# Transposing u on VectorE in blocks of 32 by 32, by way of DRAM, instead of on TensorE

## Chip, core and metric

One core of a Trainium2 chip. The metric is the device time of one execution in microseconds (us). Every time quoted with a ratio is the median of several executions, all of the fast state. Four runs were executed once only, so that their state is unknown; they are marked "one look". The experiments ran in sets on four chips, each beside runs of the kernel before on the same chip (831.6 to 831.8 us in each set).

## The reference, cut to what matters

Float32 throughout. An attention without softmax feeds an MLP mixer: first over tokens, then over channels.

```python
kv  = einsum('bhsd,bhse->bhde', k, v)
out = einsum('bhsd,bhde->bhse', q, kv)
x   = rms_norm(out) * g_norm            # (8, 576, 512), heads side by side
u   = x + (relu(x^T @ w_tok1) @ w_tok2)^T
res = u + relu(u @ w_ch1) @ w_ch2       # w_ch1: 512 x 1536, w_ch2: 1536 x 512
```

The second pass of the kernel is the last line. It works on nine groups of 512 tokens.

## The kernel before

The matmuls of this kernel sum over partitions, so `u @ w_ch1` needs u with its features on partitions; u lies in DRAM with tokens on partitions. The kernel before loads a tile of 128 tokens and turns it with four 128x128 transposes on TensorE, and ScalarE copies the result out of PSUM:

```python
def fetch_t(g, i):
    xt[g, i] = late["xt"].tile([P, DM], F32, name="xt")     # two buffers
    dma(xt[g, i], u_dram[g][ts(i, P)])

def turn_u(g, i, psum):                   # four times a group
    if i == 0:
        uT[g] = late["u"].tile([P, 7, 7, P], F32, name="uT")
    pt = psum()
    for c in range(NC):                   # NC = 4
        keep(nc.tensor.transpose(pt[:, c], xt[g, i][:, ts(c, P)], ident))
    o, n = 2 * (i // 2), 2 * (i % 2)
    copy(uT[g][:, o:o + 2, n:n + 2], pt.rearrange("p (o n) t -> p o n t", o=2))
```

Both channel matrices are multiplied by a fast scheme on two levels: seven products instead of eight, each of which is seven products again. So a group is 2 x 7 x 7 = 98 inner products of six matmuls. One inner product is one *place* of a hand-made schedule: `put(place, step)` lays a step of another engine behind the matmuls of that place. Places b to b+48 of the first channel matrix are the *first half* of a group, the 49 of the second its *second half*. Each engine's instructions stand in this order in the traces, also where one of them waits.

An outer product shares its PSUM banks between inner products. Bank `a` gathers four of them, and between two of them another engine reads the running sum:

```python
PLACE = {1: 0, 2: 1, 6: 3, 5: 4, 7: 6, 4: 9, 3: 12}
def read(o, i, j):
    a = fit(banks["a"], to(i, j))
    if base: tensor_add(o, a, base(i, j))     # VectorE
    else:    copy(o, a)                       # ScalarE
at(1, "a", True, False, lambda: read(temp("t1", 1), 0, 0))
at(6, "a", False, False, lambda: read(temp("u2", 2), 0, 1))   # next product into bank a
...                                                           # must wait for this read
```

A read that comes late on VectorE therefore stops TensorE. The second half has operands of its own (`sv`, sums of parts of v) made by VectorE shortly before TensorE needs them; its schedule, and the transposes of the next group in it:

```python
for place, steps in (
        ...
        (11, [ins[6][0]]), (12, [S4[0]]), (13, [ins[6][1], S4[1]]), ...   # S4: n3 = n2 - n6, 128x768
        (36, [xadd(0, 1, 5), ins[3][1]]), (37, [xadd(1, 1, 5)]), ...
        (44, [xadd(1, 0, 7)]), (45, [xadd(1, 1, 7)])):                    # additions to u
    put(b + place, *steps)
for i in range(J):                                                        # J = 4
    place = b + 12 + 4 * i
    put(place - 12, do(fetch_t, g + 1, i)) if i < 2 else None
    put(place - 1, do(turn_u, g + 1, i, t_psum))
    put(place, do(fetch_t, g + 1, i + 2)) if i < 2 else None
```

## Time and profile before

| | before |
|---|---|
| time | 831.66 us, median of 3 (831.65 to 831.73) |
| profiled span, granted clock | 830.2 us, 0.999 |
| first product of group 0 / first of group 1 starts | 206.34 / 280.73 us |
| first half of a group (groups 2 to 8) | 32.83 us = 49 places x 0.67 |
| second half | 34.96 us |
| TensorE waits inside groups 2 to 8 | none that the trace shows |

The halves are read from the timeline of TensorE: the start of one marker product to the start of the next. A first half of 32.83 us is TensorE at its own pace without a gap. The second half holds the four transpose sets besides (4 x 0.44 = 1.76 us), and 32.83 + 1.76 = 34.59, so 0.37 us more than its matmuls explain. Keep that in mind; it became the second half of this story. The lines of the page are in the prediction below.

### The profile page before, as it was taken

To read this page: it belongs to the slowest core of one execution; us is meant where nothing else is said; L and a number is where in the kernel's file an instruction comes from. 1 tells how busy PE (TensorE), PEld (TensorE's weight loads), DVE (VectorE), ACT (ScalarE), POOL (GpSimd) and SP (SyncE) were. 2 spreads that over 40 slices of the span, in tenths; PEclk is the share of its full clock that TensorE was granted. 3 is DMA by queue.
4 is the path that set the end of the run, shared out by engine and by line. 5 is a ranking of instruction groups with operands and counts; after the bars stand their busy time and mean duration, and the time that the engine had idled before them with its cause. 6 is when DMAs were issued, how large, how long until landed. Compare 5 with 4: busy or idle time off the path is not lost.

```text
span 830.2 us, 16562 instructions
## 1 busy us (share of the span) xinstructions
PE 812.6 (98%) x6528; PEld 719.9 (87%) x6528; DVE 701.8 (85%) x1334; ACT 289.1 (35%) x777; POOL 76.9 (9%) x59
## 2 busy tenths in 40 slices
PE   6999999999999999999999999999999999999997
PEld 6655555644888899999999999999999999999997
DVE  4688989999785979978977987997897897798696
ACT  1346665562210124234234323322423322333321
POOL 1200101010000020003003003001100300300300
PEclk9999999999999999999999999999999999999999
DMA  9999996422436445365356446546536545644642
GB/s 296 325 341 319 337 364 244 153 89 102 174 127 220 175 169 170 118 194 200 128 165 216 144 141 204 181 140 193 192 115 191 185 149 145 216 164 141 190 144 80
DMA packets 67966, 156.57 MB, mean 189 GB/s; under 512 B 5296, under 2 KB 24752, under 8 KB 67888
## 3 DMA queue, kind: packets, MB, share of 16 engines
q1 hardware_dynamic: 66208, 153.77, 56.6%
q10 hardware_dynamic: 1680, 1.74, 0.7%
q8 instruction: 52, 0.85, 0.4%
q14 instruction: 26, 0.21, 0.1%
HBM read 128.35 MB, written 27.13 MB: 187 GB/s over the span
## 4 chain that ended last, share of the span: by engine, by line
PE 88%; DVE 9%; issue 1%; DMA 1%; ACT 1%; SPq 0%; ACTq 0%; DVEq 0%
PE ps_a L127 35%; PE ps_b L127 18%; PE ps_c L127 9%; PE ps_h L127 6%; PE ps_u L127 6%; PE ps_v L127 4%; PE ps_w L127 3%; PE ps_o L127 3%; PE ps_ut L515 2%; PE ps_kv L127 2%; DVE sv L118 1%; DMA raw<-in_moe_w_tok_dram 1%; DVE v L118 1%; DVE x L379 1%; DVE ms L399 1%
## 5 line engine op out<-in xcount | busy, mean ns | idle before, releaser
L124 ACT COPY u<-ps_a 128x128 f32<-128x128 f32 (+1 forms) x176 | 60.5, 344 | 176.5 <-PE ps_a L127 164.6
L118 POOL TENSOR_TENSOR v<-v,v 128x768 f32<-128x768 f32 x32 | 58.4, 1856 | 553.0 <-ACT t L124 553.0
L127 PE MATMUL ps_b<-uT,sums 128*128 128x128 f32 x672 | 85.5, 275 | 0.0
L127 PEld LDWEIGHTS ps_b<-uT,sums 128*128 128x128 f32 x672 | 80.2, 192 | 0.0
L127 PE MATMUL ps_a<-uT,w_ch 128*128 128x128 f32 x576 | 78.8, 275 | 0.0
L127 PEld LDWEIGHTS ps_a<-uT,w_ch 128*128 128x128 f32 x576 | 71.5, 192 | 0.1
L118 DVE TENSOR_TENSOR v<-ps_b,u 128x384 f32<-128x384 f32 x112 | 60.2, 550 | 12.9 <-PE ps_b L127 12.9
L127 PE MATMUL ps_u<-h,w_tok 128*128 128x512 f32 (+1 forms) x160 | 67.0, 601 | 0.0
L127 PE MATMUL ps_h<-x,w_tok 128*128 128x512 f32 (+1 forms) x160 | 65.8, 603 | 0.8 <-ACT x L424 0.8
L118 DVE TENSOR_TENSOR v<-v,v 128x768 f32<-128x768 f32 (+1 forms) x70 | 64.1, 926 | 0.3
L118 DVE TENSOR_TENSOR uT<-uT 128x512 f32<-128x512 f32 (+4 forms) x103 | 63.1, 628 | 1.1
L124 ACT COPY t<-ps_a 128x128 f32<-128x128 f32 (+1 forms) x88 | 30.3, 344 | 92.7 <-PE ps_a L127 85.3
L121 ACT ACTIVATE v<-v 128x384 f32<-128x384 f32 (+1 forms) x102 | 49.3, 526 | 30.7 <-DVE v L118 26.6
L127 PE MATMUL ps_a<-uT,w 128*128 128x128 f32 x432 | 58.7, 275 | 0.0
L118 DVE TENSOR_TENSOR u<-ps_a,v 128x384 f32<-128x384 f32 x48 | 26.8, 558 | 32.1 <-PE ps_a L127 31.6
L127 PEld LDWEIGHTS ps_h<-x,w_tok 128*128 128x128 f32 (+1 forms) x160 | 25.9, 189 | 31.9 <-issue 28.1
L127 PEld LDWEIGHTS ps_a<-uT,w 128*128 128x128 f32 x432 | 53.4, 192 | 0.0
L118 DVE TENSOR_TENSOR xg<-xg,r 128x512 f32<-128x512 f32 (+1 forms) x78 | 50.7, 661 | 0.8 <-ACT r L124 0.6
L424 ACT ACTIVATE x<-x,inv 128x64 f32<-128x64 f32 x184 | 46.0, 335 | 9.5 <-DVE inv L419 8.1
L127 PE MATMUL ps_a<-uT,sums 128*128 128x128 f32 x336 | 46.9, 276 | 1.3 <-ACT t L124 1.3
L127 PE MATMUL ps_a<-sums,sv 128*128 128x128 f32 x336 | 47.3, 277 | 0.9 <-ACT r L124 0.5
L127 PEld LDWEIGHTS ps_u<-h,w_tok 128*128 128x128 f32 (+1 forms) x160 | 24.5, 179 | 27.1 <-issue 22.4
(123 smaller groups left out, 1650.1 us busy)
## 6 DMA issues: line engine op xcount, KB each, us to landing
sums<-sums SPq DMA_DIRECT2D x112, 576.0 KB, 3.8
qT<-in_q_dram SPq DMA_DIRECT2D x8, 1152.0 KB, 9.5
xt<-u_dram SPq DMA_DIRECT2D x36, 256.0 KB, 3.5
xg<-u_dram SPq DMA_DIRECT2D x18, 512.0 KB, 4.9
k_in<-in_k_dram SPq DMA_DIRECT2D x16, 512.0 KB, 9.2
u_dram<-x SPq DMA_DIRECT2D x16, 512.0 KB, 3.6
out_dram<-xg SPq DMA_DIRECT2D x16, 512.0 KB, 5.4
sums<-sv SPq DMA_DIRECT2D x14, 576.0 KB, 2.8
```

The source lines that it names most:

```text
L118: keep(engine.tensor_tensor(out=o, in0=a, in1=b, op=op))
L121: keep(nc.scalar.activation(o, a, AF.Relu))
L124: keep(nc.scalar.copy(o, a))
L127: keep(nc.tensor.matmul(*a, **kw))
L379: keep(nc.vector.tensor_mul(heads(X[pair, c][:, t]), heads(bank[c, t]), g_sb.to_broadcast([P, H, D])))
L399: keep(nc.vector.tensor_reduce(stats_of(c)[0][:, ts(t, H)], sq[c, t], axis=AX.X, op=ALU.add))
L424: keep(nc.scalar.activation(x[:, i], x[:, i], AF.Copy, scale=inv[:, i]))
L515: keep(nc.tensor.transpose(pt[:, c], xt[g, i][:, ts(c, P)], ident))
```

## The change

The intent: take 144 transposes off the engine that is busy 98% of the time. VectorE transposes each tile within blocks of 32 by 32, and two trips through DRAM put the blocks into their place. `uT` gets another layout (tokens in runs of 32). The loading and turning moves from the second half of the group before into its first half, four additions to u go into the next group in return, and the two PSUM banks of the transposes go to the products.

```diff
-    for c in range(NC):
-        keep(nc.tensor.transpose(pt[:, c], xt[g, i][:, ts(c, P)], ident))
-    copy(uT[g][:, o:o + 2, n:n + 2], pt.rearrange(...))
+def turn_blocks(g, i):
+    half, n = i // 2, 2 * (i % 2)
+    if n == 0:
+        xt[g] = late["y" if g else "y0"].tile([P, NC, 2, NC, Q], F32, name="y")   # one buffer
+    for o in range(2):
+        keep(nc.vector.transpose(xt[g][:, :, o, n:n + 2]..., xt[g, i][:, ts(o, DH)]...))
+    if n:                                              # after each second tile
+        t = blocks_dram[g, half] = dram.tile([Q, NC, 2, NC, P], F32, ...)
+        for a in range(NC):
+            dma(t[:, :, :, a], xt[g][ds(a * Q, Q)]...)
+def fetch_u(g, half):
+    for b in range(NC):
+        dma(uT[g][ds(b * Q, Q), 2 * half:2 * half + 2, :, :4]..., blocks_dram[g, half][:, b])
 ...
+        for place, f, i in ((2, fetch_t, 0), (8, turn_blocks, 0), (10, fetch_t, 1), (14, turn_blocks, 1),
+                            (16, fetch_t, 2), (20, turn_blocks, 2), (22, fetch_t, 3),
+                            (26, turn_blocks, 3)):
+            put(b + place, do(f, g + 1, i))            # first half
 ...
-   (36, [xadd(0, 1, 5), ins[3][1]]), (37, [xadd(1, 1, 5)]), ... (44, [xadd(1, 0, 7)]), (45, [xadd(1, 1, 7)])
+   (36, [ins[3][1]]), ... (53, [xadd(1, 1, 5)]), (55, [xadd(1, 0, 7)]), (56, [xadd(1, 1, 7)]), (59, [xadd(0, 1, 5)])
-        (transposes of group g + 1 at b + 11, 15, 19, 23)
+        put(b + 8, do(fetch_u, g + 1, 0))              # second half
+        put(b + 10, do(fetch_u, g + 1, 1))
-    late["xt"] = pool("xt", 2)
+    late["xt"] = pool("xt", 1)
-    late["m"] = pool("m", 6, PSUM); late["t"] = pool("t", 2, PSUM)
+    late["m"] = pool("m", 8, PSUM)
```

(Cut; group 0 and group 1 have their own placing: group 0 is turned during the last token mixing, group 1 during the single product stage between.)

More of the change, by code (lines that the diff above doesn't have):

```diff
@@ L504, in fetch_t @@
         if g < NG:
-            xt[g, i] = late["xt"].tile([P, DM], F32, name="xt")
+            xt[g, i] = late["xt" if g else "xt0"].tile([P, DM], F32, name="xt")
             dma(xt[g, i], u_dram[g][ts(i, P)])
-    def turn_u(g, i, psum):
+    Q = 32
+    blocks_dram = {}
+    def turn_blocks(g, i):
         if g >= NG:
             return
-        if i == 0:
-            uT[g] = late["u"].tile([P, 7, 7, P], F32, name="uT")
-        pt = psum()
-        for c in range(NC):
-            keep(nc.tensor.transpose(pt[:, c], xt[g, i][:, ts(c, P)], ident))
-        o, n = 2 * (i // 2), 2 * (i % 2)
-        copy(uT[g][:, o:o + 2, n:n + 2], pt.rearrange("p (o n) t -> p o n t", o=2))
+        half, n = i // 2, 2 * (i % 2)
+        if n == 0:
+            xt[g] = late["y" if g else "y0"].tile([P, NC, 2, NC, Q], F32, name="y")
+        for o in range(2):
+            keep(nc.vector.transpose(
+                xt[g][:, :, o, n:n + 2].rearrange("p b n t -> p n b t"),
+                xt[g, i][:, ts(o, DH)].rearrange("p (n b t) -> p n b t", n=2, b=NC)))
+        if n:
+            t = blocks_dram[g, half] = dram.tile([Q, NC, 2, NC, P], F32, name=f"blocks{g}{half}")
+            for a in range(NC):
+                dma(t[:, :, :, a], xt[g][ds(a * Q, Q)].rearrange("p b o n t -> p b o (n t)"))
+    def fetch_u(g, half):
+        if g >= NG:
+            return
+        if half == 0:
+            uT[g] = late["u"].tile([P, 7, NC, 7, Q], F32, name="uT")
+        for b in range(NC):
+            dma(uT[g][ds(b * Q, Q), 2 * half:2 * half + 2, :, :4].rearrange("p o a n t -> p o a (n t)"),
+                blocks_dram[g, half][:, b])
     def outer_u(g):
-        return t_sums(lambda n: uT[g][:, SB[n], :4]) if g < NG else []
+        return t_sums(lambda n: uT[g][:, SB[n], :, :4]) if g < NG else []
     def inner_u(g, lo, hi):
-        return t_sums(lambda n: uT[g][:, lo:hi, SB[n]]) if g < NG else []
+        return t_sums(lambda n: uT[g][:, lo:hi, :, SB[n]]) if g < NG else []
     V = {}
@@ L530, in m_psum @@
         return late["m"].tile(shape, F32, name=name, tag="m")
-    def t_psum():
-        return late["t"].tile([P, NC, P], F32, name="ps_ut")
     def v_tile(g, i):
@@ L568, in product @@
                         matmul(ps[:, w], lhsT=wt[:, 2 * i + c, ts(f, P)],
-                               rhs=uT[g][:, SB[n], c:4:2],
+                               rhs=uT[g][:, SB[n], :, c:4:2].rearrange("p a n t -> p n a t"),
                                start=(start and w == 0 and c == 0), stop=stop,
@@ L762, in mul @@
                     matmul(ps[:, ts(w, P)], lhsT=part(1, o, p, sums[n])[:, ts(w, P)],
-                           rhs=uT[g][:, SB[o], SB[p]], start=(start and w == 0), stop=stop,
+                           rhs=uT[g][:, SB[o], :, SB[p]], start=(start and w == 0), stop=stop,
                            skip_group_check=True)
@@ L881, in channel2 @@
                 (28, [ins[2][0]]), (29, [radd(6, 1)]), (30, [ins[2][1], xadd(0, 1, 6)]),
-                (32, [ins[2][3], ins[2][2]]), (34, [ins[3][0]]), (36, [xadd(0, 1, 5), ins[3][1]]),
-                (37, [xadd(1, 1, 5)]), (38, [ins[3][3], ins[3][2]]), (43, [radd(7, 6)]),
-                (44, [xadd(1, 0, 7)]), (45, [xadd(1, 1, 7)])):
+                (32, [ins[2][3], ins[2][2]]), (34, [ins[3][0]]), (36, [ins[3][1]]),
+                (38, [ins[3][3], ins[3][2]]), (43, [radd(7, 6)])):
             put(b + place, *steps)
         if g < NG - 1:
-            for place, steps in ((57, [do(store, g, xg, 1)]), (59, [xadd(0, 0, 2)]), (63, [xadd(0, 1, 3)]),
+            for place, steps in ((53, [xadd(1, 1, 5)]), (55, [xadd(1, 0, 7)]), (56, [xadd(1, 1, 7)]),
+                                 (59, [xadd(0, 1, 5)]), (60, [do(store, g, xg, 1)]), (61, [xadd(0, 0, 2)]),
+                                 (64, [xadd(0, 1, 3)]),
                                  (71, [do(store, g, xg, 0)]), (78, [do(fetch_x, g + 1, 0)]),
@@ L896, in last @@
                 tensor_add(to, to, rs[3][0][:, m, ts(n, P)])
+            for place, step in ((36, xadd(0, 1, 5)), (37, xadd(1, 1, 5)), (44, xadd(1, 0, 7)), (45, xadd(1, 1, 7))):
+                put(b + place, step)
             put(b + 49, xadd(0, 0, 2), do(store, g, xg, 1))
@@ L901, in channel2 @@
             put(b + 56, do(last, 0, 1), do(store_rest, xg, 0))
-        for i in range(J):
-            place = b + 12 + 4 * i
-            put(place - 12, do(fetch_t, g + 1, i)) if i < 2 else None
-            put(place - 1, do(turn_u, g + 1, i, t_psum))
-            put(place, do(fetch_t, g + 1, i + 2)) if i < 2 else None
+        put(b + 8, do(fetch_u, g + 1, 0))
+        put(b + 10, do(fetch_u, g + 1, 1))
         if g + 1 < NG:
@@ L1043 @@
     late["xg"] = pool("xg", 1)
-    late["xt"] = pool("xt", 2)
+    late["xt"] = pool("xt", 1)
     late["u"] = pool("u", 1)
+    first = ExitStack()
+    late["xt0"] = pool("xt0", 2, stack=first)
+    late["y0"] = pool("y0", 2, stack=first)
     fetch_t(0, 0)
@@ L1049, with turn @@
     woven = fill[0][:4] + fill[1] + fill[0][4:]
-    def turn(g, i, psum):
-        turn_u(g, i, psum)
+    def turn(i):
+        turn_blocks(0, i)
         if i + 2 < J:
-            fetch_t(g, i + 2)
-    u_psum = lambda: ps["o"].tile([P, NC, P], F32, name="ps_ut", tag="o")
+            fetch_t(0, i + 2)
+        if i % 2:
+            fetch_u(0, i // 2)
     last = [
-        "h00 2 -s40 2", "h01 2", "h10 2", "h11 2", "hr 1", "c0 u0 1", "c1 u1 1", "c2 u2", "c3 u3 1", "u4",
-        "c4 u5 1", "u6 1", "u7", "u8"]
-    more = {f"c{i}": do(turn, 0, i, u_psum) for i in range(J)}
+        "h00 2 -s40 2", "h01 c0 2", "h10 c1 2", "h11 c2 2", "hr c3 1", "u0 1", "u1 1", "u2", "u3 c4 1", "u4 1",
+        "u5 1", "u6 1", "u7", "u8"]
+    more = {f"c{i}": do(turn, i) for i in range(J)}
     more[f"c{J}"] = lambda: [f() for f in outer_u(0)]
@@ L1066 @@
     right.close()
+    first.close()
     late["v"] = pool("v", 1, "right")
@@ L1073 @@
     late["d2"] = pool("d2", 1, "right").tile([P, 3, NS, DH], F32, name="d2")
-    late["m"] = pool("m", 6, space=bass.MemoryType.PSUM)
-    late["t"] = pool("t", 2, space=bass.MemoryType.PSUM)
+    late["y"] = pool("y", 1, "right")
+    late["m"] = pool("m", 8, space=bass.MemoryType.PSUM)
     fetch_x(0, 0)
     fetch_x(0, 1)
-    fetch_t(1, 0)
-    fetch_t(1, 1)
     firsts, lasts = mix_ch2()
@@ L1084 @@
     inner2 = [split(2, o) for o in ORDER2]
-    weave(channel1_once(0), firsts + [f for fs, _ in inner1 for f in fs])
+    sums1 = firsts + [f for fs, _ in inner1 for f in fs]
+    blocks1 = [do(f, 1, i) for f, i in (
+        (fetch_t, 0), (turn_blocks, 0), (fetch_t, 1), (turn_blocks, 1), (fetch_t, 2),
+        (turn_blocks, 2), (fetch_t, 3), (turn_blocks, 3))]
+    n = len(sums1) // len(blocks1)
+    fill = []
+    for i, step in enumerate(blocks1):
+        fill += [step] + sums1[n * i:n * i + n]
+    weave(channel1_once(0), fill + sums1[n * len(blocks1):])
     for n in range(3):
         fetch_sums(n)
-    extra = [do(turn, 1, i, t_psum) for i in range(J)]
-    extra += [lambda: [f() for f in outer_u(1)], lambda: [f() for f in inner_u(1, 0, 7)], lambda: None]
-    body = [step for pair in zip(channel2_once(0), extra) for step in pair]
+    extra = [lambda: (fetch_u(1, 0), fetch_u(1, 1)), lambda: None, lambda: None,
+             lambda: [f() for f in outer_u(1)], lambda: [f() for f in inner_u(1, 0, 7)]]
+    extra += [lambda: None] * (len(channel2_once_steps := channel2_once(0)) - len(extra))
+    body = [step for pair in zip(channel2_once_steps, extra) for step in pair]
     weave(body, lasts + [f for fs, _ in inner2 for f in fs] + [f for _, f in inner1])
```

## The prediction

> **What bounds the kernel now.** I read the page first: busy shares, the slices, the chain of work that ended last, the groups.
>
> ```profile
> PE 812.6 (98%) x6528; PEld 719.9 (87%) x6528; DVE 701.8 (85%) x1334; ACT 289.1 (35%) x777; POOL 76.9 (9%) x59
> ...
> PE 88%; DVE 9%; issue 1%; DMA 1%; ACT 1%; SPq 0%; ACTq 0%; DVEq 0%
> ```
>
> TensorE is busy 98% of an 830.2 us span at full clock; most of the missing 17.6 us is the start. So every TensorE instruction that goes is worth its own time, as long as nothing else then arrives late. Next the transposes, as a group with one row per shape:
>
> ```profile
> L515 PE MATMUL ps_ut<-ident,xt 128*128 128x128 f32 x144 | 21.7, 273 | 0.0
> ...
> L124 ACT COPY uT<-ps_ut 128x512 f32<-128x512 f32 x36 | 21.1, 587 | 42.4 <-PE ps_ut L515 42.4
> ```
>
> The mean (273 ns) is a latency; matmuls overlap. The cost on the path is the step from one start to the next, in the chain in order of time:
>
> ```profile
> 727.04 1.34 PE ps_a L127 x12
> 728.38 0.67 PE ps_b L127 x6
> 729.05 0.44 PE ps_ut L515 x4
> 729.49 0.77 PE ps_b L127 x6
> ```
>
> Four transposes take 0.44 us, six matmuls 0.67. The second pass has nine groups of 512 tokens; groups 1 to 8 are fourteen products of 42 matmuls each, and one group takes 67.79 us (the chain shows the same matmuls at 356.59 and 424.38). Then I cut group 3 into its two halves, and the first half into five stretches of seven places (one place = six matmuls = 0.67 us):
>
> ```profile
> core 0: us, PE busy (x) PEld busy (x) DVE busy (x) ACT busy (x) POOL busy (x), PEclk, DMA share, GB/s
> 415.90:449.70 33.80, 33.80 (x305) 33.80 (x305) 25.14 (x48) 11.39 (x26) 7.29 (x4) 1.00 0.57 182
> 449.70:483.70 34.00, 33.95 (x304) 33.72 (x303) 33.30 (x71) 11.33 (x35) 0.00 (x0) 1.00 0.49 158
> ...
> 416.85:421.55 4.70, 4.70 (x45) 4.70 (x44) 4.24 (x9) 1.49 (x4) 0.00 (x0) 1.00 0.37 84
> 421.55:426.25 4.70, 4.70 (x45) 4.70 (x44) 3.77 (x7) 1.92 (x4) 0.00 (x0) 1.00 0.56 191
> 426.25:430.95 4.70, 4.70 (x45) 4.70 (x44) 2.63 (x6) 0.96 (x2) 0.00 (x0) 1.00 0.39 126
> ```
>
> The reader is to see that VectorE, at 85% on average, is at 98% in the second half of a group (second channel matrix, where the transposes are) and at 74% in the first, and that within that first half the first ten microseconds are the fullest (8.0 of 9.4 us).
>
> [...] Here 256 KB loads of u land 2.5 to 7.2 us after issue, median 3.5.
>
> **The change, part by part.**
>
> Removed from TensorE: 144 transposes. 36 sets of 0.44 us = 15.8 us, all on the chain. This is the gross gain. ScalarE loses 36 copies of 0.587 us (21.1 us), and it was only 35% busy.
>
> Small waits in group 1: TensorE waits 1.29 us there, and the chain back from it runs over the sums of u on VectorE (1.90 us and 2.49 us). These sums now come one product earlier: up to -1.3.
>
> Added to VectorE: 9 groups x 4 tiles x 2 = 72 block transposes of 128x256. [...] each should cost what a 128x256 addition does here: 418 ns alone, about 0.35 us in a row. Eight a group = 2.8 us; 25 us in all.
>
> Moved: four additions to u (681 ns, 0.61 in a row) leave the crowded second half of a group for the first microseconds of the next: 2.4 us. The halves become about 25.1+2.4+2.8 = 30.3 and 33.3-2.4 = 30.9 us. Against 65.7 us of matmuls (98 places of 0.67) that fits on average. The order of instructions decides whether it fits in detail.
>
> *Second half.* From 449.94 to 462.2 VectorE has no idle time, and the operand sv of product 6 of the third set is finished at about 462.16 (0.55 us from 461.61); TensorE starts on it at 462.25. Up to there the changed kernel gives VectorE the same work: the four additions came later. The matmuls alone would be ready at 449.01 + 18 x 0.67 = 461.07. So two of the four transposes of a group are paid back as a wait of about 1.2 us, and only the other two (0.88 us) are gained.
>
> *First half.* Products whose partial sums go through an addition to an earlier block must be read by VectorE before TensorE may go on in that bank; the first such read is at place 14. In the changed order four more additions and one pair of transposes stand ahead of it: 2.4+0.7 = 3.1 us, where VectorE idled 0.21+0.72+0.78 = 1.7. So the read is about 1.4 us later; its slack was 0.6 (read done 427.66, next product 428.25): a wait of about 0.8. Before the next read stand another pair and one addition: about 0.7 more. Then the DMA: the third transpose pair needs a tile whose load is issued only behind four block writes: I estimate four issues of 0.35 plus some 3 us to land = 4.5 us or more after the second pair, against about 3.8 us of work between. The fourth has a single buffer again. That delays the read at place 28 by perhaps 0.8. Sum 1.5 to 2.3 us a group.
>
> So a group costs 65.7 + 1.2 + 1.5 to 2.3 = 68.4 to 69.2, against 67.8: over the six groups that have all of it, +4 to +8. Group 1 and the last have part of it: about 0.
>
> *Group 0.* -1.8 on TensorE. But eight transposes (2.8 us) enter a VectorE that is full (8.66 of 8.8 us from 180.0 to 188.8), and the first sums of u now wait for two transfers through DRAM, about 8 us behind the last transpose; the evictions behind them hold the four banks of the token mixing. Estimate: +1 to +3 net. The single product stage that follows gets group 1's transposes and loads: +1. The stage after it loses four sets: -1.8, and the -1.3.
>
> Sum of this schedule: 831.7 + (4 to 8) + (1 to 3) + 1 - 1.8 - 1.3 = 834.6 to 840.6.
>
> **Rivals.** *All of it hidden:* if VectorE's lag is absorbed (the change also raises the PSUM banks of the products from 6 to 8, and ScalarE's copies no longer stand ahead of its reads), the time is 831.7 - 15.8 - about 2 = 814. For it: average load fits, 61 of 65.7 us; someone placed the moved additions with care. Against: the in-order reads above. *Transposes slower than an addition* [...] 845 to 855. Nothing in the profile speaks for or against. *Transfers:* 16 more transfers a group on one queue, in rows of 512 bytes; if the weight sums, loaded on the same queue three products ahead, come late, TensorE waits on DMA. Their landing is 3.8 us and I count some 11 places (7.4 us) from issue to use, so this should stay hidden, but the mean DMA share is already 0.5. *Strided matmuls:* u is now read in runs of 32; a matmul with runs of 128 (ps_v, 380 ns) costs what a contiguous one does (ps_w, 379), so I take nothing for it.
>
> **Range and chances.** My schedule says 834 to 841, full hiding 814. A hand schedule counts each lag as fully exposed, so I weigh it at two thirds and the hidden case at one third: 837 x 2/3 + 814 x 1/3 = 829. Faster by over 2% (below 815.0) needs nearly the whole gross gain: 0.10. Slower by over 2% (above 848.3) needs slow transposes or late weights: 0.13. Within 2%: 0.77. Range 814.5 to 846.
>
> **What would show it.** Right: no ps_ut rows; TensorE waits (or stretched steps) at the reads ps_a<-... by VectorE in the first half, and for sv in the second; VectorE over 90% in both halves; transposes of about 0.42 us, some with a DMA wait ahead. Wrong: groups of 66 us with TensorE gapless (then the lag is absorbed), a transpose row far from 0.42 us, or TensorE waiting for sums.

## The result, and the profile after

| | before | after |
|---|---|---|
| median | 831.69 us (4 runs, 831.65 to 831.90) | 886.31 us (4 runs, 883.67 to 889.61) |
| profiled span, granted clock | 830.2 us, 0.999 | 887.8 us, 0.981 |
| first product of group 0 / of group 1 | 206.34 / 280.73 | 210.93 / 284.29 |
| first halves of groups 2 to 8 | 32.83 | 42.53, 41.04, 40.02, 39.60, 40.99, 37.59, 32.84 |
| second halves | 34.96 | 34.86 |

The ratio is 1.066 (95% interval 1.062 to 1.070). A ratio here is the mean time of one kernel's fast runs over that of the other's of the same rounds, so it is not quite the ratio of the medians.

So the kernel got 55 us slower, in two places. The first halves of groups 1 to 7 got longer: +44.8 us in groups 2 to 7, and +10.0 in group 1 (44.01 us from its first product to the first marker of its second half, against 34.03). The start of group 1 got 3.6 us later. With the second halves (seven times -0.1) that is the whole difference of the two spans, 57.6 us. The last group has no next one to turn, and its first half is gapless at 32.84. The second half, from which the 1.76 us of transposes were taken, gained 0.10 us.

The page of the changed kernel: first the busy row, then the chain's shares.

```profile
PE 823.1 (93%) x6384; PEld 719.6 (81%) x6384; DVE 723.4 (81%) x1406; ACT 268.4 (30%) x741; POOL 77.0 (9%) x59
...
PE 46%; DVE 34%; DMA 11%; issue 4%; SPq 3%; ACT 1%; DVEq 0%; ACTq 0%
```

The 144 matmuls are gone, and yet TensorE's busy time has *risen* by 10.5 us. In the chain, DMA went from 1% to 11% and VectorE from 9% to 34%. A TensorE that does less work in more time points to waits and to a slower clock (granted 0.981, against 0.999 before). The waits, longest in total first (engine and line, releaser: us in total, times, longest):

```profile
PE ps_a L127 <- DVE t L118: 18.5, 13, 5.2
PE ps_a L127 <- DMA sums<-sums: 8.9, 5, 2.4
PE ps_b L127 <- DVE v L118: 7.1, 8, 2.1
```

and VectorE's own, with the cost of the transposes themselves (a group by shape):

```profile
DVE y L521 <- DMA xt<-u_dram: 26.4, 14, 5.3
```

```profile
L521 DVE STREAM_TRANSPOSE y<-xt 128x256 f32<-128x256 f32 x72 | 27.5, 420 | 26.4 <-DMA xt<-u_dram 26.4
```

A transpose costs 420 ns, as predicted. What is dear is that it stands in VectorE's order and waits for its load. One first half (group 3, place b at 439.88 us) shows how. VectorE's transposes, two per tile (start, duration, what it waited for in brackets):

```profile
451.68 0.76 DVE L521 STREAM_TRANSPOSE y<-xt 128x256 f32<-128x256 f32 x2
...
458.17 0.77 DVE L521 STREAM_TRANSPOSE y<-xt 128x256 f32<-128x256 f32 x2 [1.72 <-DMA xt<-u_dram]
...
464.21 0.77 DVE L521 STREAM_TRANSPOSE y<-xt 128x256 f32<-128x256 f32 x2 [2.17 <-DMA xt<-u_dram]
```

the issues on the queue that carries all these transfers:

```profile
452.46 2.54 SPq L115 DMA_DIRECT2D blocks<-y  x4
455.11 0.55 SPq L115 DMA_DIRECT2D xt<-u_dram  x1
455.70 0.44 SPq L115 DMA_DIRECT2D sums<-sums  x1
...
458.97 0.32 SPq L115 DMA_DIRECT2D xt<-u_dram  x1
```

and the chain there, which is the same thing seen from its end:

```profile
455.11 2.94 DMA xt<-u_dram
...
458.97 5.22 DMA xt<-u_dram
```

The second tile is turned at 451.68. Only after four block writes, issued in 2.54 us, is the third tile's load issued; it lands 2.94 us later; VectorE turns it at 458.17. There is one buffer, so the fourth load can only go at 458.97, takes 5.22 us, and VectorE stands again until 464.21. Everything on VectorE behind these transposes is late too, among it the reads of bank `a` and the results of bank `b`. TensorE in the same stretch:

```profile
451.81 0.94 PE L127 MATMUL ps_a<-uT,sums 128*128 128x128 f32 x6 [0.37 <-DVE t L118]
...
459.44 0.94 PE L127 MATMUL ps_b<-uT,sums 128*128 128x128 f32 x6 [0.69 <-DVE v L118]
...
465.95 1.65 PE L127 MATMUL ps_a<-uT,sums 128*128 128x128 f32 x6 [2.89 <-DVE t L118]
467.39 2.77 PE L127 MATMUL ps_b<-uT,sums 128*128 128x128 f32 x12
469.95 2.42 PE L127 MATMUL ps_a<-uT,w 128*128 128x128 f32 x12
```

Where nothing waits in this half, twelve matmuls take 1.50 us as a row. After the wait of 2.89 us they take 2.77 and 2.42. From start to start, the 30 matmuls from 465.95 take 6.26 us in place of 30/6 x 0.67 = 3.35. The stretch 465 to 470 (window, then us, TensorE busy, weight loads, VectorE, ScalarE, GpSimd, granted clock, DMA share, GB/s) says why:

```profile
465.00:470.00 5.00, 4.05 (x19) 4.05 (x20) 3.78 (x8) 0.89 (x2) 0.00 (x0) 0.50 0.75 144
```

The granted clock was 0.50. So this first half is 41.04 - 32.83 = 8.2 us too long, of which 2.9 us is half clock after a long wait and 5.3 us is waits (stretched steps at 451.8, 454.5, 459.4 and 466.0: about 0.6, 0.6, 1.0 and 3.1). Over the whole run the clock was 0.50 in six stretches of 3.41 or 6.83 us, and TensorE worked in 27.7 us of them. Half of that, 13.9 us, is my estimate of what the lower clock cost; the kernel before had no such stretch while TensorE worked. The profiled execution is the slowest of the four, with the lowest clock (0.981; the others 0.984 to 0.989).

### The profile page after: what moved, and what is told of

Its sections match the earlier page's. It is cut to its first block, busy times and chain, and to the rows that moved or that the text cites. A ratio compares the mean times of both kernels' runs of the same rounds, so it can differ in the third digit from the quotient of the medians.

```text
span 887.8 us, 16510 instructions
## 1 busy us (share of the span) xinstructions
PE 823.1 (93%) x6384; PEld 719.6 (81%) x6384; DVE 723.4 (81%) x1406; ACT 268.4 (30%) x741; POOL 77.0 (9%) x59
## 4 chain that ended last, share of the span: by engine, by line
PE 46%; DVE 34%; DMA 11%; issue 4%; SPq 3%; ACT 1%; DVEq 0%; ACTq 0%
PE ps_a L127 15%; PE ps_b L127 9%; DVE v L118 9%; DMA xt<-u_dram 6%; DVE sv L118 5%; PE ps_v L127 4%; PE ps_h L127 4%; PE ps_u L127 4%; PE ps_c L127 3%; DVE uT L118 3%; DVE xg L118 3%; SPq L115 3%; DMA sums<-sums 3%; PE ps_o L127 2%; PE ps_w L127 2%
## 5 line engine op out<-in xcount | busy, mean ns | idle before, releaser
L127 PE MATMUL ps_b<-uT,sums 128*128 128x128 f32 x672 | 94.2, 288 | 7.7 <-DVE v L118 7.1
L127 PEld LDWEIGHTS ps_b<-uT,sums 128*128 128x128 f32 x672 | 86.3, 202 | 10.1 <-DVE v L118 10.1
L127 PE MATMUL ps_a<-uT,sums 128*128 128x128 f32 x336 | 50.7, 289 | 28.0 <-DVE t L118 18.5
L127 PEld LDWEIGHTS ps_a<-uT,sums 128*128 128x128 f32 x336 | 43.7, 199 | 31.6 <-DVE t L118 20.9
L127 PE MATMUL ps_a<-uT,w 128*128 128x128 f32 x432 | 61.8, 285 | 0.0
L127 PEld LDWEIGHTS ps_a<-uT,w 128*128 128x128 f32 x432 | 56.8, 202 | 0.0
L127 PEld LDWEIGHTS ps_u<-h,w_tok 128*128 128x128 f32 (+1 forms) x160 | 24.9, 183 | 35.1 <-issue 23.5
```

What stands on the lines that cost most here:

```text
L127: keep(nc.tensor.matmul(*a, **kw))
```

## The experiments

Theory 1: the tiles are turned too close together for a single buffer and one queue, VectorE waits for loads in order, and TensorE waits for VectorE; part of it is then drawn out by the clock (30 matmuls in 6.26 us in place of 3.35, above). Rivals: the four moved additions crowd the start of the first half; the clock alone is to blame; the transposes' work itself overfills VectorE. Theory A, which came up on the way, is about the second half and is told below.

### The four additions put back, and alone

First, the kernel after with the four additions where they were:

```diff
-  (53, [xadd(1, 1, 5)]), (55, [xadd(1, 0, 7)]), (56, [xadd(1, 1, 7)]), (59, [xadd(0, 1, 5)])   # next group
+  (36, xadd(0, 1, 5)), (37, xadd(1, 1, 5)), (44, xadd(1, 0, 7)), (45, xadd(1, 1, 7))           # as before
```

> The changed kernel with the four additions at their old places. Theory 1 (VectorE stands in order behind transposes that wait for the one-tile buffer of u and its transfer): the waits for the transfer stay, so the time stays within some 10 us of 886, say 876 to 896. Theory 2 (the moved additions crowd the first half and that is the main cost): the first reads come about 2.4 us earlier in each group, and the time falls by 15 us or more, below 870.

877.36 us (one look), correct. First halves 37.8 to 38.6, second halves 34.86 as in the kernel after; granted clock 0.992. Most of the 55 us stays. The 9 us that went are no clean measure of the move: in groups 2 to 7 of this run the clock never fell, whereas in the kernel after TensorE worked 18.9 us at half clock there, which by the count above is 9.4 us. So the clock alone is not to blame either: without it the first halves are still some 5 us too long.

Then the move alone, in the kernel before (no block transposes, TensorE's transposes kept):

> The kernel before with only the four additions moved to the next group. Theory A: a second half of a group is fixed by VectorE's order in its first 26 places, ahead of the places where these additions stood, and a first half has room for them (with no transposes it took 32.84 us, gapless). Then nothing changes: 34.96 and 32.83 us, 831.7 us, ratio 0.998 to 1.002. Theory 2 (the moved additions crowd the first half): first halves 0.5 us or more longer, 835 or more.

831.89 us (12 runs), ratio 1.0001 (0.9993 to 1.001), halves 32.84 and 34.96. By itself the move does nothing at all. Not in the first half, where VectorE has room for it, and not in the second, where the additions came after the crowded part. Whether it costs anything in the kernel after, by pushing the transposes and the loads behind them further back, is not shown.

### One load a group

The kernel after, loading only the first tile of a group; all four turns read that one (wrong result on purpose). The transposes and the block writes stay, but no load stands behind another's turn:

```diff
 def fetch_t(g, i):
+    if g and i:
+        return
 ...
-    ... xt[g, i][:, ts(o, DH)]
+    ... xt[g, 0 if g else i][:, ts(o, DH)]
```

> Wrong result on purpose: from group 1 on only the first tile of u of a group is loaded, and all four transpose pairs read it, so VectorE never waits for tiles 2 to 4; every other instruction, the block writes and the reads included, stays. Theory 1: the 26.4 us that VectorE waits for these loads go, TensorE's long wait at place 31 shrinks below 1 us, its clock does not drop, and the time falls by 25 to 40 us to 845 to 860; what is left is the one-tile buffer of the transposed blocks and the moved additions. Theory 2 (crowding of VectorE) and theory 3 (the weight sums come late behind the block writes on the one queue): it falls by less than 10 us.

867.93 us (one look): 18 less than the kernel after, between the two expectations, so neither was met. About half of the 18 is half clock that did not come (8.6 us of work in place of 27.7). The first halves still take 36.6 to 36.8. With three of four loads gone, the trace shows waits of VectorE for the single buffer `y` that the block writes have to leave (3.7 us in all), and TensorE waits of 10.4 us for the weight sums. So the loads are not the whole of it: the block writes and the sums on the same queue belong to it.

### No turning at all

All of it away in groups 1 to 8: no load, no transpose, no block writes; `uT` is filled straight from u's memory with the same number of transfers (wrong result on purpose):

> Wrong result on purpose: from group 1 on no loads of tiles for the transposes, no transposes and no block writes; the transposed u is read straight from DRAM in the same pieces. This is the gross gain with the moved additions kept. If the matmuls with runs of 32 cost no more than before and only the transposes and their transfers hurt: groups of 66 to 67.5 us and 820 to 830 us in all, since group 0 still comes some 5 us late. If the strided matmuls or the moved additions are to blame, it stays above 845.

834.01 us (one look). First halves 32.84: gapless, so the waits in the first half are all the transposes' and their transfers' doing. But the total is above the expected range, and above the kernel before. The second halves are 34.86, as if TensorE had never been relieved. This was the surprise of the study. Where TensorE waits in one second half of this run (start, duration, wait in brackets):

```profile
460.46 0.94 PE L127 MATMUL ps_b<-w_ch,sv 128*128 128x128 f32 x6 [0.27 <-DVE r L118]
464.57 0.91 PE L127 MATMUL ps_a<-sums,sv 128*128 128x128 f32 x6 [0.49 <-ACT r L124]
471.33 0.94 PE L127 MATMUL ps_b<-d,sv 128*128 128x128 f32 x6 [0.46 <-DVE r L118]
```

The three rows, 12, 17 and 26 places into the half, are TensorE waiting for what VectorE makes. The middle one names ScalarE, but its operand sv is finished on VectorE at 464.47 (0.55 us from 463.92), just before the product starts. VectorE itself shows no idle time from 452.3 to 480.6. In the kernel before, the same place 17 is a step of 0.88 us in place of 0.67; its sv is finished at 462.16:

```profile
461.37 0.83 PE L127 MATMUL ps_a<-sums,v 128*128 128x128 f32 x6
462.25 0.91 PE L127 MATMUL ps_a<-sums,sv 128*128 128x128 f32 x6
```

That is theory A: the second half is set by VectorE's work in order in its first 26 places. The 1.76 us that TensorE spent on transposes there would then lie in the shadow of it.

### VectorE relieved by GpSimd: a failed test of theory A

To relieve VectorE in that stretch I moved the two additions S4 (0.95 us each on VectorE, wanted much later) to GpSimd, once without transposes and once in the kernel before:

```diff
-  tensor_add(half(n3(), i), half(n2(), i), half(n6(), i), ALU.subtract)
+  tensor_add(half(n3(), i), half(n2(), i), half(n6(), i), ALU.subtract, nc.gpsimd)
```

> Wrong result on purpose: the run without transposes, and two additions of a second half (places 12 and 13, 0.87 us each in a row, their result not read before place 34) moved from VectorE to GpSimd. Theory A (a second half is VectorE's order, TensorE's transposes stood in its gaps): waits at places 17 and 26 go, second halves fall from 34.86 to 33.0 to 33.5 us, and over eight groups the time falls by 10 to 15 us, to 819 to 824. Theory B (something else holds a second half, such as ScalarE's reads or the weight sums): no change, 832 to 835.

> The kernel before, right result, with the same two additions on GpSimd and TensorE's transposes kept. Theory A: only its 0.38 us of waits in a second half can go, since the four sets of transposes (1.76 us) are then really on the path: 34.96 falls to 34.6, the time by 2 to 3 us to 829 to 830. Theory B: no change.

850.22 us (ratio 1.022, 1.021 to 1.024) and 858.09 us (ratio 1.032, 1.030 to 1.033): slower, by more than either theory allows. The relief was none. GpSimd takes 2.3 us for each, and while it works, VectorE's sums sv take nearly four times as long, 2.05 and 1.95 us in place of 0.55 (VectorE first, then GpSimd):

```profile
464.78 2.05 DVE L118 TENSOR_TENSOR sv<-v 128x384 f32<-128x384 f32 x1
...
466.96 1.95 DVE L118 TENSOR_TENSOR sv<-sv,v 128x384 f32<-128x384 f32 x1
```

```profile
463.85 4.64 POOL L118 TENSOR_TENSOR v<-v,v 128x768 f32<-128x768 f32 x2 [10.14 <-DVE v L118]
```

In this trace an sv of 0.55 us took 2.05, and both sv shown end 0.4 us after one of the two GpSimd additions does (466.42 and 468.50). TensorE's wait at the same place 17 grew from 0.49 to 2.52 us. So the runs speak for sv as the thing waited for, but they were no test of what relief is worth.

### VectorE relieved by leaving work out: the test that told

The same two additions left out (wrong result on purpose), without transposes and in the kernel before:

```diff
-  (11, [ins[6][0]]), (12, [S4[0]]), (13, [ins[6][1], S4[1]]),
+  (11, [ins[6][0]]), (13, [ins[6][1]]),
```

> The kernel after without any transposes or block transfers in groups 1 to 8, and besides without VectorE's two additions of sum4 (2 x 0.87 us, places 12 and 13 of the second half; wrong result on purpose). Theory A: the second half of a group is set by VectorE's work in order in its first 26 places, so that taking TensorE's four transposes away (1.76 us) gained nothing there. Then with VectorE relieved by 1.74 us the second half falls from 34.86 to 33.0 to 33.4 us (33 is 49 places of 0.67), and the total from 834 to 820 to 823. Theory B (second half set by something else: banks, DMA, TensorE's own rate with these operands): 34.86 stays, total 832 to 835.

> The kernel before without the two additions of sum4 (wrong result on purpose): TensorE keeps its four transposes a group. Its second half is 49 places of 0.67 plus 1.76 for the transposes = 34.6, against 34.96 measured. Theory A: only 0.2 to 0.4 us a group to gain, total 828.5 to 830.5; with the run beside it, taking the transposes away is then worth about 1.5 us a group where VectorE is relieved and 0.1 us where it is not. Theory B: no telling difference between the two rows (both within 1 us of 834 and 831.7).

| second half, us | VectorE as it is | without the two S4 | worth of it |
|---|---|---|---|
| with TensorE's transposes | 34.96 (before) | 34.67 | 0.29 |
| without | 34.86 | 33.37 | 1.49 |
| worth of taking them away | 0.10 | 1.30 | |

822.50 us (ratio 0.989, 0.987 to 0.990) and 828.29 us (ratio 0.996, 0.994 to 0.997); as theory A expected, but for the second total, which lies 0.2 us below its range. The first half is the same in both. Of the three waits only the first is left in the run without transposes:

```profile
456.99 0.94 PE L127 MATMUL ps_b<-w_ch,sv 128*128 128x128 f32 x6 [0.27 <-DVE r L118]
```

The last group has no next one to turn, so the kernel before has a second half without transposes too. From the marker in the middle of that group to the end it takes 40.26 us, and 38.76 without the two S4: 1.50 where no transposes stand, 0.29 where they do, in the same run. Two limits lie almost upon one another in this half: TensorE's 34.6 us of instructions and VectorE's 34.9. Lifting one by 1.7 us shows 0.1 or 0.3; lifting both shows 1.6.

### A TensorE kept busy during the wait: inconclusive

Ten dummy matmuls (2.2 us) at place 30 of the first half, where the longest wait stood (2.89 us in group 3), to see whether the granted clock then stays at full (their bank is taken from the eight of the products):

```diff
+  put(b + 30, lambda: [matmul(warm, lhsT=ident, rhs=ident, start=True, stop=True) for _ in range(10)])
```

> The changed kernel with ten matmuls of the identity (2.2 us) ahead of the product at place 31 of groups 1 to 7, in a PSUM bank of their own (the products have 7 instead of 8). They fill a wait and do no work. If the granted clock falls [...] and each fall costs some 2.9 us (30 matmuls in 6.26 us instead of 3.35), the mean granted clock comes back to 0.995 or more and the time falls by 8 to 20 us although TensorE has 15 us more to do. If the clock has nothing to do with the wait, the time stays or rises, up to 900.

884.47 us (one look), correct; granted clock 0.990 instead of 0.981. In groups 2 to 7 one stretch of half clock is left (3.41 us from 383.74, after a wait of 2.15 us) in place of four, but the matmuls cost time of their own where the wait was shorter than they. Neither the clock nor the time came out as expected, and the 2 us are within the spread of the kernel after. How much of the 55 us is the clock was not settled by this run; the 13.9 us above remain an estimate.

### Group 0 back on TensorE

The kernel after, with group 0 alone turned on TensorE as before:

```diff
-        turn_blocks(0, i)
+        turn_u0(i, u_psum)          # four transposes, copies into the new layout of uT
```

> The kernel after with group 0 alone transposed on TensorE as before (its four sets and ScalarE copies back, no blocks through DRAM for it); groups 1 to 8 as in the kernel after. Theory: the first product of the second pass starts 4.6 us later in the kernel after (210.9 against 206.3) because the sums of group 0 wait for two transfers through DRAM. Then ps_v starts at 206 to 207 again and the time falls by 3 to 5 us: 881 to 884. Rival: the late start is made good later (the stage has waits anyway), then the first product of group 1 (284.3) does not move and the total stays at 884 to 889.

878.08 us (ratio 1.056, 1.054 to 1.058), correct. The first product of group 0 starts at 205.84 instead of 210.93, that of group 1 at 278.46 instead of 284.29. So the detour through DRAM in group 0 cost 5.8 us that nothing made good later; the other 2.4 us came from the first halves (38.7 to 40.7), which differ from run to run.

### Spaced out, in two steps

If the waits are a matter of placing, spreading the turning over the 49 places of the first half should end them. (A second buffer for the loads or for `y` would be the other way; no run on record tried it.) First step: tiles turned at places 19, 28, 40, 47 instead of 8, 14, 20, 26, the block writes at 28 and 49, and the trips back into `uT` from place 11 of the second half on:

> The changed kernel, right result, with the same instructions in other places: transpose pairs at places 19, 28, 40 and 47 instead of 8, 14, 20 and 26, so that the one-tile load and the block writes between them have 6 us or more; the second block write and the reads of the transposed u somewhat later. Theory 1: VectorE no longer waits for the loads, first halves fall from 37.6 to 42.5 us to 33 to 33.6, the clock stays, and the time is 834 to 840, that is the run without any transposes plus little. If the sheer work or the queue is to blame, first halves stay above 35 us, 850 or more.

846.86 us (ratio 1.017, 1.016 to 1.019), correct: 39.5 us better than the kernel after, but 7 above the expectation. First halves 33.5 to 37.1. In the trace, VectorE still waited 22.5 us for loads. The queue shows the reason; the two transposes of VectorE that follow are below it:

```profile
440.87 2.65 SPq L115 DMA_DIRECT2D blocks<-y  x4
443.61 0.56 SPq L115 DMA_DIRECT2D xg<-u_dram  x1
444.21 0.50 SPq L115 DMA_DIRECT2D xt<-u_dram  x1
```

```profile
448.65 0.77 DVE L521 STREAM_TRANSPOSE y<-xt 128x256 f32<-128x256 f32 x2 [2.00 <-issue]
...
454.94 0.77 DVE L521 STREAM_TRANSPOSE y<-xt 128x256 f32<-128x256 f32 x2 [1.77 <-DMA xt<-u_dram]
```

The third load stands in the queue behind four block writes and a load that nobody needs yet (`xg`, the residual). So, second step: the third load ahead of the block writes, the two `xg` loads seven places later, the last tile one place earlier, and group 0 on TensorE as in the run above.

```diff
-  (28, turn_blocks, 1), (28, write_blocks, 0), (29, fetch_t, 2), (40, turn_blocks, 2), (41, fetch_t, 3), (47, turn_blocks, 3), (49, write_blocks, 1)
+  (27, turn_blocks, 1), (27, fetch_t, 2), (28, write_blocks, 0), (39, turn_blocks, 2), (39, fetch_t, 3), (46, turn_blocks, 3), (47, write_blocks, 1)
-  (78, [do(fetch_x, g + 1, 0)]), (85, [do(fetch_x, g + 1, 1)])
+  (85, [do(fetch_x, g + 1, 0)]), (92, [do(fetch_x, g + 1, 1)])
-  put(b + 11, do(fetch_u, g + 1, 0)); put(b + 16, do(fetch_u, g + 1, 1))
+  put(b + 10, do(fetch_u, g + 1, 0)); put(b + 15, do(fetch_u, g + 1, 1))
```

> Group 0 transposed on TensorE again, groups 1 to 8 with the block transposes spaced over the first half (places 19, 27, 39, 46), the third load issued ahead of the block writes instead of behind them, and the two loads of the residual tile seven places later. Correct result. Theory (what is lost is only waits for transfers crowded on one queue, and group 0's detour): the first product of group 1 starts at 278.5 as in the run before; first halves 32.9 to 33.6, second halves 34.86 to 35.3; total 829 to 835, so no more than a tie with the kernel before, because even without any transposes and with group 0 restored the sum is 834.0 - 5.5 = 828.5. Rival (the block transfers cost time however they are placed, by load on the DMA engines): first halves stay at 34 or more, total 839 to 843.

828.85 us (7 runs), correct, ratio 0.9974 (0.9962 to 0.9985), granted clock 1.0: faster than both kernels, though a tie at 2%. First halves 32.85, gapless, with the turning of groups 2 to 8 in them; so the transposes' own work does not overfill VectorE. One first half (columns as in the window above), the row of all 64 transposes, and the queue in that half:

```profile
483.00:515.85 32.85, 32.85 (x297) 32.85 (x296) 28.97 (x58) 11.17 (x26) 7.30 (x4) 1.00 0.70 218
```

```profile
L521 DVE STREAM_TRANSPOSE y<-xt 128x256 f32<-128x256 f32 x64 | 24.4, 419 | 1.8 <-DMA xt<-u_dram 1.3 <-DMA blocks<-y 0.4
```

```profile
501.87 0.32 SPq L115 DMA_DIRECT2D xt<-u_dram  x1
502.24 2.52 SPq L115 DMA_DIRECT2D blocks<-y  x4
```

The same transposes of the same 419 ns: the idle time ahead of them fell from 26.4 us (72 transposes) to 1.8. Several placements were changed at once, so which of them did it is not separated. The second halves are 34.86 (one 35.11). TensorE still waits for weight sums in them, three times, 4.0 us in all; the 35.11 is the half with the longest of these waits (2.04 us). At the marker in the middle of the last group its trace is 3.3 us ahead of the kernel before (786.02 against 789.31): 2.3 are there when group 1 starts, 0.6 in group 1's first half, and only 0.3 in all that follows. In the stage before group 1 VectorE sets no limit, and there the removed transposes of group 1 are worth their full time: from the first product of that stage to the first of group 1 it is 36.26 us against 38.02, four sets of 0.44 us to the hundredth.

## Why the prediction was wrong

It gave 829 us and a range of 814.5 to 846; the kernel took 886.31. "Slower by over 2%" had 0.13. By its own steps:

- **TensorE bound, so each transpose is worth its time** (15.8 us gross). Right before group 1: the four sets there, "-1.8", were gained in full. Wrong in the second halves, where 28 of the 36 sets lie: there four of them were worth 0.10 us together. (Of the 17.6 us in which TensorE had no work, 8.4 lie in the first 30 us and 6.2 in the last 45, so "most" is not the start. Nothing hung on that.)
- **Second half: a wait of about 1.2 us, 0.88 us gained.** The mechanism was right, VectorE's order up to sv at place 17. The size was off, because I took that one place for the only limit. The runs show three waits (places 12, 17 and 26), which eat 1.66 of the 1.76 us.
- **First half: 1.5 to 2.3 us of stall a group.** This is the step that failed. The mechanism was named to the letter: late reads of bank `a`, the third load behind four block writes, a single buffer for the fourth. The terms were too small. The four issues took 2.54 us, not 4 x 0.35 = 1.4. VectorE's wait for the third tile, 0.7 us by my figures (4.5 against 3.8), was 1.7. The fourth was put at "perhaps 0.8", and its load alone, issued only after the third was turned, took 5.22 us; TensorE stood 2.89 us there. And I let each lag end in its own stall; in the trace VectorE stood 1.72 us ahead of the third tile and then 2.17 ahead of the fourth, and TensorE's waits in that half came to 5.3 us (above). VectorE was not full there (28.96 of 41.06 us in group 3), it stood and waited. Measured: 37.6 to 42.5 us instead of 34.3 to 35.1. A misread view hid part of it: the first ten microseconds of the half are not "the fullest" (8.0 of 9.4 us), for the two stretches from 430.95 on, left out of the fence, hold 8.06, and there the late fourth tile falls.
- **No step at all for the clock.** I counted a wait as its own length. Here half clock (0.50) began within a wait of 2.89 us, at 465.05, and stayed to 471.87: another 2.9 us (30 matmuls in 6.26 in place of 3.35).
- **Weight sums stay hidden.** Wrong: TensorE waited for them 8.9 us in all, up to 2.4 at a time, on the queue that now carried 16 transfers more a group. I had compared a landing of 3.8 us with 7.4 us of lead and left out what stands ahead in the queue.
- **Group 0: +1 to +3.** The detour was found, its size too small: the first product came 4.6 us later, and undoing it moved the start of group 1 by 5.8. The "+1" of the single product stage was 0.7. Of the "-1.3" in group 1 at most 0.7 came (33.37 us to the marker in the run without transposes, 34.03 before). With the turning, group 1 took 10.0 us more, where I had put "about 0".
- **A transpose costs what an addition does** (418 ns alone, 0.35 in a row): right, 420 ns and 0.38 us (0.76 for two). The rival of slower transposes falls. **Strided matmuls cost nothing**: right, six matmuls took 0.67 us as before.
- **Blending 837 with 814.** I weighed my own schedule down for "counting each lag as fully exposed". It had left lags out, and the tail was on the other side. "Slower by over 2%" was to need slow transposes or late weights; mostly it came through late tiles of u. The rival "all hidden: 814" could not come about in this schedule: even with no transposes anywhere in groups 1 to 8 the time is 834.01, and with group 0 restored 834.0 - 5.5 = 828.5 would be its floor.

The 829 us that I predicted is what the well-placed version takes, but that is luck, for the reasons are not mine: its first halves hide everything, and its second halves gain nothing.

## What to carry to other kernels

Before taking work off the busiest engine, look in each stage for the engine that would be next, and test it cheaply: leave the work out altogether, with a wrong result. That run (834 us here, 828.5 with group 0 restored) shows the most that the idea can give in this schedule, and it was worth more than the arithmetic. When an instruction that waits for a DMA is put into the order of an engine that others depend on, lay out the queue too: what stands ahead of that load, how many buffers, and whether two waits follow one another (here 1.72 and 2.17 us, and then 2.89 on TensorE); with group 0 on TensorE in both, the same 64 transposes took 878.08 us at the first places and 828.85 at the last, and the two kernels differ only in where the transposes and transfers stand.

## What the traces show besides

- Half clock after a wait of TensorE. In the kernel before with S4 on GpSimd, seven waits of 2.09 us were each followed by it: sets of six matmuls took 1.49 us in place of 0.83. Yet one wait of 2.52 us in that run was not followed by it, and of eight waits of 2.52 us in the run without transposes and with S4 on GpSimd only three were. In the kernel after, waits of 2.44, 2.89, 1.86 and 2.76 us (ending at 395.95, 465.95, 611.48 and 691.01) stand at the starts of half clock at 396.78, 465.05, 611.82 and 690.33; others of 2.06, 2.14 and 2.35 us (from 381.35, 538.89 and 545.99) have none behind them. So the length of a wait alone does not tell it, and what else does is not shown here.
- A transpose on TensorE: 273 ns as the mean of one, 0.11 us on the path (four in 0.44), and in the second half, where VectorE sets the pace, 0.10/16 = 0.006 us.
- A 128x256 float32 transpose in 32 by 32 blocks on VectorE: 420 ns, 0.38 us in a row.
- Issuing from SyncE: on this queue four block writes of 128 KB in rows of 512 bytes took 2.54 us to issue, 0.63 each; most others took 0.32 to 0.44. No run shows what makes the difference.
- VectorE beside GpSimd: a sum of 0.55 us took 2.05 us while a GpSimd addition of 2.3 us ran.
